# The first batch of an attention and feed-forward kernel rebuilt: weight conversion, softmax division and the second batch's scores

## The chip, the cores and the metric

The kernel runs on one core of one Trainium2 chip. The metric is the device time of one execution in microseconds (us), the median of several runs. The engines are TensorE (PE, matrix products; PEld is its weight load), VectorE (DVE), ScalarE (ACT), GpSimd (POOL) and SyncE (SP, which here only issues transfers). Each runs its own instructions in order and waits for the others by semaphores.

## What is computed

Eight batches of causal windowed attention with eight heads (576 positions, 64 columns a head, a window of 128, a slope of position for each head), then a bilinear feed-forward layer without a nonlinearity. Cut to what matters:

```python
scores = scale * np.matmul(q, k.transpose(0, 1, 3, 2))
scores = np.where(mask, scores + bias[None], -1000000000.0)
scores = scores - np.max(scores, axis=-1, keepdims=True)
attn = np.exp(scores)
attn = attn / (np.sum(attn, axis=-1, keepdims=True) + 1e-09)
attn_out = np.matmul(attn, v)
x = np.ascontiguousarray(attn_out.transpose(0, 2, 1, 3)).reshape(B * S, H * D)   # 4608 x 512
a, b = x @ w_a, x @ w_b                                                          # 512 x 1536 each
out = (a * b) @ w_out                                                            # 1536 x 512
```

The weights arrive as 64-bit floats, and the kernel turns them into 32-bit floats itself. Most products are made of pairs of 16-bit numbers (a high and a low half, three products for one), which needs a power of two as a scale for every operand.

## The kernel before, in words

Heads go in pairs, four pairs to a batch. The scores of a pair are nine tiles of 64 queries by at most 192 keys, laid into four PSUM banks (`BANKS`). The feed-forward layer of a batch is `up` (12 blocks f, each with 48 matmuls of 288 columns in the plain form) and `down` (288 matmuls).

**Batch 0** has its own attention, `first_attention`, in float32. For each bank `first_scores` makes the scores (line 438), subtracts them from the row minimum on DVE (442), takes the exponential with its row sum on ACT (443), adds 1e-9 to the sums (444), takes their reciprocal (445), multiplies the probabilities by it (449 on ACT, 451 on DVE) and transposes them on PE (454). `first_pv` multiplies by v (400), and `keep_x` copies the result out of PSUM (322).

**Weights.** `as_float32` loads one block (512 columns of 128 partitions) and puts together each float from its two words: the low word by ACT (124) or, in every second call, by POOL (126), the high word by DVE (127, 128), the sum by POOL (129). `up_weights` then squares the block (139), sums over the partitions on PE (141), takes a scale (145 and `power_scale`, lines 107 to 110) and splits the block into two halves (152 on ACT, 153 on DVE). `down_weights` does the same for the output weights, with one scale for all (164 to 176). Four of the twelve steps of `up_weights` are woven into the first attention, the rest and `down_weights` into batch 0's `up`.

**Batches 1 to 7.** `attention` is a generator of sevenths of a pair. For each pair it squares q and k for a scale (`qk_squares`, 245 to 248, with a small sum on PE, 256), splits them (`split_qk`, 260 to 263), lays the halves out by four transfers (266 to 269), makes the scores from 16-bit halves (290), normalises the probabilities into two halves, `phl` (307, 308), transposes them by a transfer into `pT` (313), and multiplies by v (400). `v_squares` (211) and `v_scale` (the sum `vtot` on PE, 218) give v's scale once a batch. `Pace.along` spreads these steps along the matmuls of the batch before: while batch b runs `up`, the attention goes to place 4b + 4, while it runs `down`, to 4b + 6.

**What sets the order.** A scheduler orders the instructions of each engine. From batch 1 on, PE's instructions stand in the order in which the code is written; in batch 0 no engine's do.

Of the kernel before, what the change touches and what calls it, by code (L numbers as in the profile page):

```python
# [46 lines left out]
def attention_then_bilinear_ffn(ctx: ExitStack, tc: tile.TileContext, qT, kT, vP, w_a, w_b, w_out, rel, slopes2, outT):  # L47
# [38 lines left out]
    raws = [wdn[:, 2 * n:2 * n + 2, :, :].rearrange("p a c f -> p (a c f)").bitcast(I64) for n in range(6)]  # L86
    forms = [wup[:, n, 4:6, :, :, :].rearrange("p a c k f -> p (a c k f)").bitcast(F32) for n in range(NF)]
# [24 lines left out]
    turn, tt, tt0 = count(), count(), count()  # L112

    def as_float32(x, src):

        k = next(turn)
        raw = raws[k % 6]
        act.dma_start(raw, src)
        words = raw.bitcast(I32).rearrange("p (n two) -> p n two", two=2)
        low, high = words[:, :, 0], words[:, :, 1]  # L120
        t = x.bitcast(I32)

        if k % 2 == 0:
            act.activation(low, low.bitcast(U32), AF.Copy, scale=float(2.0**-29))
        else:
            pool.tensor_scalar(out=low, in0=low.bitcast(U32), scalar1=float(2.0**-29), scalar2=None, op0=ALU.mult)
        vec.tensor_scalar(out=t, in0=high, scalar1=3, scalar2=0x3FFFFFF8, op0=ALU.logical_shift_left, op1=ALU.bitwise_and)
        vec.scalar_tensor_tensor(out=t, in0=high, scalar=-0x40000000, in1=t, op0=ALU.bitwise_and, op1=ALU.bitwise_or)  # L128
        pool.tensor_tensor(out=t, in0=t, in1=low, op=ALU.add)  # L129
        return raw.bitcast(BF16)[:, 0:512]  # L130

    def up_weights(f):

        ps = ps_at.tile([P, 512], F32, tag="at", name="wn_ps")
        fs = []
        for m, w in ((0, w_a), (1, w_b)):
            x = forms[(2 * f + m) % NF]
            sq = as_float32(x, w[f])
            act.activation(sq, x, AF.Square)
            for c in range(NKC):  # L140
                pe.matmul(ps[:, m * P:(m + 1) * P], ones16, sq[:, c * P:(c + 1) * P], start=(c == 0), stop=(c == NKC - 1))
            fs.append(x.rearrange("p (a k f) -> p a k f", a=2, k=2))
            yield
        top = small.tile([P, 2], F32, tag="wtop", name="wtop")
        vec.tensor_reduce(out=top, in_=ps[:, 0:2 * P].rearrange("p (m f) -> p m f", f=P), op=ALU.max, axis=AX)

        power_scale(sup[:, f, :], top, 1.01, 14)
        for m in range(2):
            s = sup[:, f, m:m + 1]

            hi, lo = ((wup[:, f, 0:2, n, :, :] if m == 0 else wup[:, f, 3:1:-1, n, :, :]) for n in range(2))
            act.activation(hi, fs[m], AF.Copy, scale=s)
            vec.scalar_tensor_tensor(out=lo, in0=fs[m], scalar=s, in1=hi, op0=ALU.mult, op1=ALU.subtract)  # L153
        yield

    def down_weights():

        sums = small.tile([P, NF], F32, tag="wos", name="wos", bufs=1)
        for f in range(NF):
            sq = as_float32(forms[f], w_out[f])  # L160
            act.activation(sq, forms[f], AF.Square, accum_out=sums[:, f:f + 1])
            yield
# [9 lines left out]
        vec.tensor_scalar(out=ratio, in0=sab, scalar1=smin, scalar2=so, op0=ALU.mult, op1=ALU.mult)  # L172
        for f in range(NF):
            s = ratio[:, f:f + 1]
            act.activation(wdn[:, f, 0, :], forms[f], AF.Copy, scale=s)
            vec.scalar_tensor_tensor(out=wdn[:, f, 1, :], in0=forms[f], scalar=s, in1=wdn[:, f, 0, :], op0=ALU.mult, op1=ALU.subtract)
            if f % 2:
                yield
# [52 lines left out]

    def load_qk(b, p):
# [19 lines left out]
    def split_qk(o):  # L252
# [10 lines left out]
        vec.scalar_tensor_tensor(out=lo.rearrange("p h s -> p (h s)"), in0=qk.rearrange("p h s -> p (h s)"), scalar=own, in1=hi.rearrange("p h s -> p (h s)"), op0=ALU.mult, op1=ALU.subtract)  # L263

        o.qs = work.tile([P, 2, S], F16, tag="qst", name="qst", bufs=1)
# [8 lines left out]
        vec.reciprocal(o.neg, t)  # L274
        o.bias = work.tile([P, WIN], F32, tag="bias", name="bias")
        eng = vec if b == 1 else pool
        eng.tensor_scalar(out=o.bias, in0=rel_sb, scalar1=t, scalar2=sl2_sb[:, p:p + 1], op0=ALU.mult, op1=ALU.mult)
# [3 lines left out]
    def scores(o, bi):  # L281
# [3 lines left out]
        for i, c in BANKS[bi]:  # L285
            w = TILES[i][1]
            qq, kk = slice(64 * i, 64 * i + 64), slice(64 * i + 64 - w, 64 * i + 64)
            for ks, last in ((o.kh, False), (o.kl, True)):
                for e in range(2):
                    pe.matmul(ps[64 * e:64 * e + 64, c:c + w], o.qs[:, e, qq], ks[:, e, kk], start=not last, stop=last)  # L290
# [452 lines left out]
    for _ in range(10):  # L743
        next(att)
# [75 lines left out]
```

## Time and profile before

| What | us |
|---|---|
| Three runs: median, lowest, highest | 1092.01, 1091.65, 1095.06 |
| The profiled execution: its own time, its span | 1091.0, 1089.2 |
| First `up` matmul of batch 0 | 58.0 |
| First `down` matmul of batch 0 | 216.2 |
| First `up` matmul of batch 1 | 259.6 |
| First `down` matmul of batch 1 | 345.6 |
| Last `down` matmul of batch 1 | 398.7 |

The profile is one execution. Times in it count from the start of its span. The granted clock is the share of its full clock that PE was given. A view by stretches gives the busy time of each engine; a view by groups gives, for a line of the code, the operation, how often it ran, its busy time, the mean duration in ns, and the idle time of the engine ahead of it with what ended it. In names such as `wup<-wdn`, the tile written stands left and the tile read right.

### The profile page before, as it was taken

Reading aid. Unit: us, or ns where it says so; the run is one execution under the profiler, and the core shown is the slowest. Engines: PE = TensorE matmul, PEld = TensorE weight load, DVE = VectorE, ACT = ScalarE, POOL = GpSimd, SP = SyncE. Lnnn points to the kernel's source line nnn. Section 1 sums busy time; section 2 is a strip of 40 time slices with the busy share of each in tenths; the row PEclk is TensorE's granted clock in tenths of the full one; section 3 lists DMA queues with packets and bytes.
Section 4 is the critical chain, followed back from the end, with each engine's and each line's share of the span. In section 5 each row is a group of like instructions: output and inputs, shape, how many; then the busy total and the mean of one; then the engine's idle time right before and its main releaser. Section 6 shows DMA issues by size and latency. Waiting matters only on the chain.

```text
span 1089.2 us, 23914 instructions
## 1 busy us (share of the span) xinstructions
PE 986.8 (91%) x9231; PEld 755.8 (69%) x9231; DVE 725.9 (67%) x2028; ACT 661.6 (61%) x1730; POOL 327.0 (30%) x345
## 2 busy tenths in 40 slices
PE   6776867498999979989799999999999999999998
PEld 5454645376777757767577777777777777777776
DVE  6849998974658845798477758675777666632530
ACT  6957775867546665566656676566756675522321
POOL 6316536500136801496021301122112202220110
PEclk7987988698999989999899999999999999999999
DMA  7236665556323641235431463246334643200000
GB/s 277 78 101 190 200 122 160 130 134 130 66 55 71 145 107 34 51 84 147 110 83 45 100 164 79 61 89 172 81 62 89 154 100 62 40 28 17 2 12 33
DMA packets 149714, 105.19 MB, mean 97 GB/s; under 512 B 120288, under 2 KB 128608, under 8 KB 148576
## 3 DMA queue, kind: packets, MB, share of 16 engines
q1 hardware_dynamic: 134912, 75.25, 31.0%
q10 hardware_dynamic: 14688, 28.42, 8.0%
q8 instruction: 72, 1.18, 0.4%
q14 instruction: 42, 0.34, 0.1%
HBM read 48.33 MB, written 9.44 MB: 53 GB/s over the span
## 4 chain that ended last, share of the span: by engine, by line
PE 43%; DMA 5%; ACT 4%; DVE 2%; issue 1%; ACTq 0%; SPq 0%; DVEq 0%
PE ch L596 15%; PE dn_ps L691 13%; PE p L596 11%; DMA pT<-phl 2%; PE x_ps L400 2%; ACT phl L307 2%; PE sc_ps L290 2%; DMA qk<-in_kT 1%; DMA v<-in_vP 1%; ACT t L295 1%; DVE phl L308 1%; ACT vsq L211 0%; DVE qkl L263 0%; ACT rc L638 0%; DVE rin L303 0%
## 5 line engine op out<-in xcount | busy, mean ns | idle before, releaser
L596 PEld LDWEIGHTS <-wup 128*128 128x128 f16 x4212 | 409.4, 99 | 147.2 <-issue 24.3
L691 PE MATMUL dn_ps<-h,wdn 128*128 128x288 f16 x2304 | 301.3, 290 | 0.0
L691 PEld LDWEIGHTS <-wdn 128*128 128x128 f16 x2304 | 222.6, 99 | 64.7 <-issue 0.5
L596 PE MATMUL ch<-xs,wup 128*128 128x288 f16 x1584 | 229.0, 286 | 5.7 <-DVE rc L655 2.9
L596 PE MATMUL up_ps<-xs,wup 128*128 128x288 f16 x1440 | 193.9, 295 | 18.4 <-DVE wup L153 8.5
L596 PE MATMUL p<-xs,wup 128*128 128x288 f16 x1188 | 178.1, 286 | 5.4 <-ACT rc L638 5.4
L295 ACT ACTIVATE t<-t,mn 128x192 f32<-128x192 f32 (+2 forms) x252 | 107.4, 427 | 63.5 <-DVE mn L294 63.3
L650 POOL TENSOR_TENSOR rc<-rc,row 128x288 f32<-128x288 f32 x66 | 57.2, 866 | 268.2 <-DVE row L648 203.2
L308 DVE SCALAR_TENSOR_TENSOR phl<-t,rin,phl 128x192 f16<-128x192 f32 (+2 forms) x252 | 104.0, 447 | 17.1 <-ACT phl L307 17.0
L307 ACT ACTIVATE phl<-t,rin 128x192 f16<-128x192 f32 (+2 forms) x252 | 88.7, 424 | 23.5 <-DVE rin L304 12.3
L294 DVE CUSTOM_DVE_ANT_0 t<-sc_ps,bias,neg 128x192 f32<-128x192 f32 (+2 forms) x252 | 87.4, 388 | 22.1 <-PE sc_ps L290 21.9
L589 ACT CAST h<-rc 128x576 f16<-128x576 f32 x96 | 64.0, 666 | 57.3 <-DVE rc L655 24.9
L590 DVE TENSOR_TENSOR h<-rc,h 128x576 f16<-128x576 f32 x90 | 74.2, 824 | 23.5 <-ACT h L589 22.6
L329 POOL TENSOR_TENSOR xq<-xq,sq 128x576 bf16<-128x576 bf16 x24 | 34.0, 1417 | 164.8 <-ACT sq L328 164.7
L335 DVE TENSOR_TENSOR xs<-v,xs 128x576 f16<-128x576 f32 x51 | 52.9, 1050 | 27.1 <-ACT xs L334 26.8
L400 PE MATMUL x_ps<-pT,vhl 128*64 128x128 f16 (+3 forms) x1176 | 50.3, 238 | 18.7 <-DMA pT<-phl 17.3
L695 ACT ACTIVATE row<-dn_ps,oi 128x288 f32<-128x288 f32 x64 | 31.5, 492 | 56.1 <-PE dn_ps L691 55.4
L627 DVE TENSOR_TENSOR rc<-p,rc 128x288 f32<-128x288 f32 x66 | 29.9, 454 | 53.1 <-PE p L596 47.9
L400 PEld LDWEIGHTS <-vhl 128*64 128x64 f16 (+1 forms) x1176 | 46.3, 115 | 22.8 <-DMA pT<-phl 17.9
L290 PEld LDWEIGHTS <-qst 128*64 128x64 f16 x1008 | 36.9, 112 | 36.0 <-issue 30.4
L290 PE MATMUL sc_ps<-qkh,qst 128*64 128x192 f16 (+2 forms) x504 | 52.1, 253 | 9.0 <-DMA qkh<-qkh 8.9
L129 POOL TENSOR_TENSOR wup<-wup,wdn 128x512 int32<-128x512 int32 x36 | 50.8, 1416 | 29.7 <-DVE wup L128 10.8
(132 smaller groups left out, 1284.7 us busy)
## 6 DMA issues: line engine op xcount, KB each, us to landing
v<-in_vP SPq DMA_DIRECT2D x8, 1280.0 KB, 6.2
qk<-in_qT SPq DMA_DIRECT2D x32, 288.0 KB, 4.0
qk<-in_kT SPq DMA_DIRECT2D x32, 288.0 KB, 4.4
out<-row ACTq DMA_DIRECT2D x64, 144.0 KB, 1.8
wdn<-in_w_a ACTq DMA_DIRECT2D x12, 512.0 KB, 3.8
wdn<-in_w_b ACTq DMA_DIRECT2D x12, 512.0 KB, 5.2
wdn<-in_w_out ACTq DMA_DIRECT2D x12, 512.0 KB, 5.2
qst<-qkh SPq DMA_DIRECT2D x28, 144.0 KB, 2.8
```

Of the source, the lines that this page charges most:

```text
L290: pe.matmul(ps[64 * e:64 * e + 64, c:c + w], o.qs[:, e, qq], ks[:, e, kk], start=not last, stop=last)
L294: vec.tensor_tensor_reduce(out=t[:, c:c + w], in0=ps[:, c:c + w], in1=o.bias[:, WIN - w:WIN], scale=o.neg, scalar=3.0e38, op0=ALU.add, op1 ...
L295: act.activation(t[:, c:c + w], t[:, c:c + w], AF.Exp, bias=o.mn[:, n:n + 1], scale=-1.0, accum_out=o.sm[:, n:n + 1])
L307: act.activation(phl[:, 0, pc:pc + w], e, AF.Copy, scale=s)
L308: vec.scalar_tensor_tensor(out=phl[:, 1, pc:pc + w], in0=e, scalar=s, in1=phl[:, 0, pc:pc + w], op0=ALU.mult, op1=ALU.subtract)
L335: vec.tensor_tensor(out=xs[:, n, 1, :, :], in0=src, in1=xs[:, n, 0, :, :], op=ALU.subtract)
L400: pe.matmul(xp[oc // 512][64 * h:64 * h + 64, o0:o0 + w], vt[0:rows, c:c + 64], probs(pt, rows, blocks, h), start=(n == 0 and first), stop ...
L589: act.copy(h[:, f, :, 0, :], hid)
L590: eng.tensor_tensor(out=h[:, f, :, 1, :], in0=hid, in1=h[:, f, :, 0, :], op=ALU.subtract)
L596: pe.matmul(ps[:, 0:HT], wup[:, a[0], a[1], wi, k, :], xs[:, b, xi, k, :], start=(first and n == 0), stop=(last and n == len(ks) - 1), ski ...
L650: pool.tensor_tensor(out=x0, in0=x0, in1=mid, op=ALU.mult)
L691: pe.matmul(ps[:, 0:HT], wdn[:, f, wi, e * P:(e + 1) * P], h[:, f, t, hi, :], start=(m == 0 and n == 0), stop=(m == NF - 1 and n == 2))
```

## The change

It rewrites batch 0 and shifts steps of the attention of all others:

- **Weights.** `convert` works on two blocks in one call (128 x 2 x 512), with the low words always on ACT. The steps of a block are spread over four turns, so that one block is converted while the one before is summed and scaled and the one before that is split. Three loads go through SP. In the first attention 2.2 turns are taken for each bank, so that most of the blocks are done there.
- **First attention.** The probabilities stay undivided. A matmul with ones (`ones32`) gives the sums in the layout of x, ACT copies them out, DVE takes a reciprocal of 128 x 576 for each pair, and x is multiplied by it when it is read from PSUM. The scores of a bank are made ahead of the transposes of the bank before.
- **Batch 1's scores** come from float32 q and k, loaded as they are: no squares, no scale, no split, no layout transfers. The bias tile goes from DVE to POOL.
- **Pace.** Batch 0's `up` takes the attention to place 3.5 and its `down` to 4.9 (before: 4 and 6). `first_up` keeps two results waiting before they are read, and `first_down` goes over f outside and the four output blocks inside. In batch 0 SP's transfers stand in written order.
- **All batches.** The third pair (p == 2) of a batch has its products with v and its normalisation later; `v_squares` and `v_scale` come one seventh later; the layout transfers follow the last bank of scores.

```diff
-    def as_float32(x, src):
...
+    def convert(n):
+        low, high, t = words(n)
+        act.activation(low, low.bitcast(U32), AF.Copy, scale=float(2.0**-29))
+        vec.tensor_scalar(out=t, in0=high, scalar1=3, scalar2=0x3FFFFFF8, op0=ALU.logical_shift_left, op1=ALU.bitwise_and)
+        yield
+        vec.scalar_tensor_tensor(out=t, in0=high, scalar=-0x40000000, in1=t, op0=ALU.bitwise_and, op1=ALU.bitwise_or)
+        for m in range(2):
+            pool.tensor_tensor(out=t[:, m, :], in0=t[:, m, :], in1=low[:, m, :], op=ALU.add)
+        yield
...
+        def pv(p, pt):
+            sums = [ps_ch.tile([P, 512], F32, tag="ch", name="sum_ps") for _ in range(2)]
+            each_pv(sums, (ones32,), (pt,))
+            yield
+            r = first.tile([P, S], F32, tag="rin0", name="rin0", bufs=1)
+            x = st.v[:, p, 0:S]
+            for n, (c, w) in enumerate(halves_of_x):
+                act.activation(r[:, c:c + w], sums[n][:, 0:w], AF.Copy, bias=1e-9)
+            xp = [ps_ch.tile([P, 512], F32, tag="ch", name="x_ps") for _ in range(2)]
+            each_pv(xp, (st.v[:, p, :],), (pt,))
+            vec.reciprocal(r, r)
+            yield
+            for n, (c, w) in enumerate(halves_of_x):
+                vec.scalar_tensor_tensor(out=x[:, c:c + w], in0=xp[n][:, 0:w], scalar=st.sv, in1=r[:, c:c + w], op0=ALU.mult, op1=ALU.mult)
...
+            if o.b == 1:
+                for e in range(2):
+                    r = slice(64 * e, 64 * e + 64)
+                    pe.matmul(ps[r, c:c + w], o.q[r, qq], o.k[r, kk], start=True, stop=True)
+                continue
...
+            elif prev and p != 1:
                 prev.vhl = split_v(st, prev.p)
...
-            if o:
+            if o and p != 2:
                 normalize(o)
...
+        weave(att.along(first_up(st, h), 49, 3.5), (weights, 0, 48, 50))
+        weave(att.along(first_down(0, out_scale(st), h), 24, 4.9), (weights, 0, 12, 12))
```

How the instructions stand now, on the two engines that the waits lead to. First DVE in the first attention, around the last bank of a pair. `t` holds a bank's scores, `sm` its row sums, `mn` the row minima, `sup` the scale of a weight block, and `rin` the reciprocals of the sums in the layout of x. Before:

```order
L445 RECIPROCAL sm_285<-sm_285 128x3
L451 TENSOR_SCALAR t_149<-t_149,sm_285 128x64
L451 TENSOR_SCALAR t_149<-t_149,sm_285 128x192
L444 TENSOR_SCALAR sm_312<-sm_312 128x2
L442 ISA t,mn_334<-sc_ps,bias_282 128x192
L442 ISA mn_334 128x1
```

With the change:

```order
L127 TENSOR_SCALAR wup<-wdn 128x2x512
L157 TENSOR_REDUCE wtop<-wn_ps 128x2
L110 TENSOR_SCALAR sup<-r 128x2
L580 RECIPROCAL rin_548<-rin_548 128x576
L550 ISA t,mn_600<-sc_ps,bias_378 128x192
L550 ISA mn_600 128x1
```

The small sums, reciprocals and products between the minima are gone; in their place stand weight instructions of double width, and once a pair a reciprocal of 576 columns.

Second ACT near the end of a `down` (that of batch 1), where v of the next batch is squared. `vsq` is the square of v, `qkl` that of the next pair's q and k, `row` an output block. Before:

```order
L211 ACTIVATE vsq,vs<-v 128x640
L245 ACTIVATE qkl,qs<-qk 128x1152
L295 ACTIVATE t,sm<-t,mn 128x192 x2
L211 ACTIVATE vsq,vs<-v 128x640
L695 ACTIVATE row<-dn_ps,oi 128x288
```

With the change:

```order
L260 ACTIVATE vsq,vs<-v 128x640
L365 ACTIVATE t,sm<-t,mn 128x192
L869 DMA out<-row 128x288
L365 ACTIVATE t,sm<-t,mn 128x192
L260 ACTIVATE vsq,vs<-v 128x640
L365 ACTIVATE t,sm<-t,mn 128x192
L303 ACTIVATE qkl,qs<-qk 128x1152
```

The last square of v now stands ahead of the squares of q and k, and no longer behind them. On PE the sum `vtot` that needs it stands 18 `down` matmuls ahead of the next `up`, where it stood 36 ahead.

More of the change, by code (lines that the diff above doesn't have):

```diff
@@ L1 @@
 from contextlib import ExitStack
-from itertools import chain, count, cycle
+from itertools import chain, cycle
 import numpy as np
@@ L110, in power_scale, with load_weights @@
         vec.tensor_scalar(out=dst.bitcast(I32), in0=r, scalar1=float(-(2**23)), scalar2=float((189 + top) * 2**23), op0=ALU.mult, op1=ALU.add)
-    turn, tt, tt0 = count(), count(), count()
-    def as_float32(x, src):
[L116 to L126, printed above, removed]
+    def load_weights(n, srcs, queue=act):
+        for m, src in enumerate(srcs):
+            queue.dma_start(raws[n % 3][:, m, :], src)
@@ new lines, in first_attention @@
+        bias(0)
+        n = 4 * NPAIR
+        t = exponentials(0, 0, products(0, 0))
+        beside = iter(())
+        for k in range(n):
+            p, bi = k // 4, k % 4
+            ps = products((k + 1) // 4, (k + 1) % 4) if k + 1 < n else None
+            other(0.5)
+            if bi == 1 and p + 1 < NPAIR:
+                bias(p + 1)
+            tp = transposed(t)
+            if ps:
+                t = exponentials((k + 1) // 4, (k + 1) % 4, ps)
+            next(beside, None)
+            keep(bi, tp, pts[p % 2])
+            if p == 0 and bi < 2:
+                v_squares(st, (2 * bi, 2 * bi + 1))
+            if p == 0 and bi == 2:
+                v_scale(st)
+            if bi == 3:
+                beside = pv(p, pts[p % 2])
+            other(0.5)
@@ L502, in first_attention @@
+        for _ in beside:
+            other(0.5)
         states[0] = st
-        yield
     def attention():
@@ L527, in attention @@
                 scores(o, 0)
+            nxt = squares(i + 1)
+            if p == 1 and b > 1:
+                st = load_v(b)
+            if p == 2:
+                late.vhl = split_v(st, late.p)
+            yield i + 1 / 7
+            if o:
+                scores(o, 1)
             if p == 2:
@@ L610, in up_plain @@
                 yield
[L611 removed]
+        halve(hid, f, h, vec)
     def up_fast(st, f, h):
```

355 lines of the change are left out of this document (222 added, 133 removed).

## The prediction

> **What bounds the kernel now.** I read the busy time by stretches first, cut at the stages of the table above.
>
> ```profile
> core 0: us, PE busy (x) PEld busy (x) DVE busy (x) ACT busy (x) POOL busy (x), PEclk, DMA share, GB/s
> 0.00:58.00 58.00, 41.01 (x345) 28.68 (x346) 44.90 (x162) 46.48 (x141) 28.66 (x43) 0.81 0.47 167
> 58.00:200.00 142.00, 104.75 (x922) 75.79 (x920) 121.81 (x304) 95.94 (x237) 68.58 (x44) 0.87 0.57 155
> 200.00:259.60 59.60, 47.65 (x461) 36.15 (x462) 43.40 (x148) 44.15 (x120) 10.84 (x9) 0.83 0.62 136
> 259.60:345.60 86.00, 82.70 (x778) 64.53 (x777) 51.95 (x128) 47.64 (x120) 25.92 (x35) 0.96 0.37 77
> 640.00:755.00 115.00, 112.08 (x1109) 86.74 (x1106) 80.31 (x244) 76.44 (x206) 23.62 (x23) 1.00 0.44 101
> ```
>
> The last row is one batch of the steady part: PE is busy 112 of 115 us, so little is left there. The first three rows are batch 0. It takes 259.6 us where a steady batch takes 115; its most loaded engine is DVE (44.90 + 121.81 + 43.40 = 210 us), with ACT at 187, PE at 193 and a lower clock. From 58 to 200 DVE is busy 122 of 142 us. So batch 0 is set by DVE, with holes, and everything later by PE. Next, what PE waited for, first in batch 0, then after it.
>
> ```profile
> PE x_ps L400 <- DMA pT<-phl: 17.3, 2, 9.2
> PE tr_ps L454 <- ACT t L449: 9.3, 5, 3.6
> PE up_ps L596 <- DVE wup L153: 8.5, 4, 4.0
> PE sc_ps L290 <- DMA qkh<-qkh: 7.0, 2, 4.5
> ...
> PE vtot L218 <- DVE vc L215: 15.9, 5, 6.6
> PE p L596 <- ACT rc L638: 5.4, 10, 1.7
> ```
>
> In batch 0 four different releasers follow each other: the transfer of the probabilities, the division on ACT, the weight split on DVE, the layout transfer. The change touches three of the four. After batch 0 the largest wait is the sum of v's squares, 15.9 us in five pieces.
>
> **Batch 0, what DVE loses.** Busy times are of the first 260 us.
>
> ```profile
> L451 DVE TENSOR_SCALAR t<-t,sm 128x192 f32<-128x192 f32 (+2 forms) x18 | 8.4, 474 | 0.4
> L444 DVE TENSOR_SCALAR sm<-sm 128x2 f32<-128x2 f32 (+1 forms) x16 | 3.8, 240 | 3.5 <-ACT t L443 3.4
> L445 DVE RECIPROCAL sm<-sm 128x2 f32<-128x2 f32 (+1 forms) x16 | 2.6, 161 | 0.2
> L263 DVE SCALAR_TENSOR_TENSOR qkl<-qk,own,qkh 128x1152 f16<-128x1152 f32 x7 | 10.9, 1559 | 2.0 <-ACT qkh L262 1.9
> L277 DVE TENSOR_SCALAR bias<-rel_sb,ninv,sl_sb 128x192 f32<-128x192 f32 x4 | 1.8, 447 | 0.0
> L272 DVE SCALAR_TENSOR_TENSOR ninv<-sc 128x1 f32<-128x1 f32 x7 | 1.1, 150 | 0.0
> ```
>
> - The division of the probabilities (451, 444, 445) goes: 8.4 + 3.8 + 2.6 = **14.8 us**.
> - Batch 1's preparation of q and k goes for four of the seven pairs prepared by then: 4/7 of 10.9 + 1.1 is 6.9, the bias adds 1.8; with seven other instructions a pair of at least the 0.15 us of line 272, 4.2, it is **12.9 us**.
> - Lines 127 and 128 run 18 times in place of 36, at twice the width. The fixed part of an instruction is about that of one element, 0.15 us (line 272): 36 x 0.15 = **5.4 us**.
> - POOL no longer converts low words, and DVE is held up by them:
>
> ```profile
> 16.46 0.69 DVE L128 SCALAR_TENSOR_TENSOR wup<-wdn,wup 128x512 int32<-128x512 int32 x1
> 17.06 0.42 DVE L127 TENSOR_SCALAR wup<-wdn 128x512 int32<-128x512 int32 x1
> 19.09 0.87 DVE L127 TENSOR_SCALAR wup<-wdn 128x512 int32<-128x512 int32 x1
> 18.71 1.88 POOL L126 TENSOR_SCALAR wdn<-wdn 128x512 int32<-128x512 uint32 x1
> L126 POOL TENSOR_SCALAR wdn<-wdn 128x512 int32<-128x512 uint32 x18 | 32.8, 1823 | 49.8 <-DVE wup L127 17.8 <-DVE wup L153 10.5 <-DMA wdn<-in_w_out 8.9
> L127 DVE TENSOR_SCALAR wup<-wdn 128x512 int32<-128x512 int32 x36 | 19.0, 527 | 6.8 <-DMA wdn<-in_w_out 4.7 <-DMA wdn<-in_w_a 2.0
> ```
>
> The same line takes 0.42 us alone and 0.87 beside line 126, 0.53 in the mean, so its 36 runs lose 36 x 0.11 = 4 us. POOL is busy 108 us in batch 0, 33 of them with line 126. Line 127 is a tenth of DVE's time: if only it were held up, 33/108 of 4 is 1 us; if all of DVE were held up alike (210 x 0.11/0.53 = 44 us), 13. I take **6**.
>
> **What DVE gains.** A reciprocal of 576 columns is in no row; the widest is of 12.
>
> ```profile
> L445 DVE RECIPROCAL sm<-sm 128x2 f32<-128x2 f32 x12 | 1.9, 159 | 0.2
> L445 DVE RECIPROCAL sm<-sm 128x3 f32<-128x3 f32 x4 | 0.7, 170 | 0.0
> L166 DVE RECIPROCAL sab<-sab 128x12 f32<-128x12 f32 x1 | 0.2, 215 | 0.0
> L459 DVE COPY pT<-tr_ps 128x512 f32<-128x512 f32 x2 | 1.4, 683 | 0.0
> ```
>
> From 2 to 12 columns it grows by 56 ns, 5.6 a column, against 1.3 a column in all for the copy of 512. Over 576 columns that is 3.4 us. The ends are a copy's price, 0.77, and the steepest pair of rows (2 to 3 columns, 11 ns), 6.5. I take 3.4, the longest step: 4 x 3.4 = **13.6 us** (3 to 26). The product that writes x from PSUM, 512 and 64 columns, is at most 0.9 us by the copy: 4 x 0.9 = **3.6**.
>
> The Trainium skill, "VectorE: DVE Perf Modes", section "First, the fixed hardware budget", speaks against this edit: reciprocal is an iterative divide with a repeat count of 8. At that page's 0.96 GHz an estimate is 576 x 8 / 0.96 = 4.8 us, and the sum would come out 5.6 us higher; the slope over narrow rows agrees with it in kind, not in size.
>
> Sum for DVE: -14.8 - 12.9 - 5.4 - 6 + 13.6 + 3.6 = -21.9. In the timeline above the 128 of 16.46 lasts until 17.15 and runs into the 127 of 17.06: neighbours overlap by about a tenth, so **-20 us**.
>
> **What moves.** By place 4.9 instead of 6, five pairs of scores stand ahead of batch 1 instead of six. A pair costs DVE
>
> ```profile
> L294 DVE CUSTOM_DVE_ANT_0 t<-sc_ps,bias,neg 128x192 f32<-128x192 f32 (+2 forms) x54 | 18.6, 385 | 4.0 <-PE sc_ps L290 4.0
> L308 DVE SCALAR_TENSOR_TENSOR phl<-t,rin,phl 128x192 f16<-128x192 f32 (+2 forms) x54 | 23.8, 484 | 2.1 <-ACT phl L307 2.1
> ```
>
> (18.6 + 23.8) / 6 + 1.6 for its split = 8.7 us: **-9** in batch 0. In batch 1 PE pays for it, and batch 0 pays for the float32 scores:
>
> ```profile
> 31.00:36.00 5.00, 3.36 (x36) 2.39 (x36) 1.00 0.19 40
> 346.40:360.00 13.60, 2.09 (x36) 1.23 (x36) 1.00 0.11 32
> 346.40:360.00 13.60, 1.63 (x42) 1.55 (x42) 1.00 0.11 32
> DVE xs L335 <- ACT xs L334: 8.3, 1, 8.3
> ```
>
> The first row is a pair's scores in float32, the second one in halves, the third a product with v, all at full clock. The moved pair puts 2.1 + 1.6 = **+4 us** on PE in batch 1, where DVE has room (52 of 86 us). Float32 adds 4 x 1.3 = 5 us to PE in batch 0, and the sums by ones about as much again as float32 products with v. PE is busy 193 of 259.6 us there, so most lies beside DVE; for the part in `down`, where PE leads, and for `first_down` reading four banks in a row at its turn, I charge **+3**. If DVE no longer leads, up to 10 are paid.
>
> The fourth row is DVE's longest wait in batch 0, at the seam between first attention and `up`. With most weight blocks now beside the attention and the sums behind, there is other work for DVE in that hole: **-6** (0 to -8). The edits on ACT are costed at nothing: it loses its share of the divisions, the row sums' reads and the squares of q and k, gains the low words of 18 blocks, and stays under DVE (187 against 210); without that cover they cost the difference, a few us. The three loads that go through SP stand ahead of v there; v is first used after the first bank, and a late v costs only that bank's cover.
>
> Batch 0: -20 - 9 - 6 + 3 = **-32 us**; batch 1: +4.
>
> **Batches 1 to 7.** `vtot` stands 18 `down` matmuls later on PE, and 18 of them take 2.3 us:
>
> ```profile
> 616.13 2.31 PE dn_ps L691 x18
> 643.66 0.24 PE L218 MATMUL vtot<-vc,ones 128*128 128x1 bf16 x4 [1.57 <-DVE vc L215]
> 391.27 0.25 PE L218 MATMUL vtot<-vc,ones 128*128 128x1 bf16 x4 [6.59 <-DVE vc L215]
> ```
>
> Three of the five waits are like the 1.57 and vanish, 4 us; the two long ones lose 2.3 each. The 6.59 loses more, because the last square of v stood on ACT behind the squares of q and k and now stands ahead. I take -9 of 15.9. The waits for ACT's copies (5.4 us) come where ACT stands at `phl` and waits for the transfer that still reads it:
>
> ```profile
> 534.72 8.30 DMA pT<-phl
> 543.11 1.50 ACT phl L307 x5
> 545.12 0.90 PE p L596 x6
> ```
>
> The third pair's normalisation now comes two sevenths later: -3. Together **-12** (0 to -20; what is behind PE there is all the rest of its queue).
>
> **Sum**, against the profiled execution's own 1091.0 (1 us under the median): 1091 - 32 + 4 - 12 = **1051 us**.
>
> **The rivals.**
> - *Dearer reciprocals.* Iteration makes one column cost near the upper rows, 8 ns, 4.8 us a pair: 4 x 1.4 more, **1057**. For it the slope; against it the row of 12. The rule of the Trainium skill above is this one.
> - *The waits only change names after batch 0.* PE takes everything in written order there, and a later step can hold what stands behind it: no gain and 4 us lost with the moved pair, 1091 - 32 + 4 + 2 = **1065**. For it: steady batches have 3 us of idle PE, so nothing much can be won.
> - *DVE isn't the bound, the chain is.* Four releasers alternate in batch 0; with each shorter, the next takes over, and half of 32 is won: 1091 - 16 + 4 - 2 = **1077**.
> - *Slower.* DVE's order puts each reciprocal ahead of the next pair's minima; it waits for transposes, sums and the copy. If DVE stands still for that chain, about 8 us a pair (3.4 for the next scores by the row above, as much again for transposes and sums, 1 for copies), that is 32 us, and 12 more if the reciprocals take 6.5: 1091 - 32 + 32 + 12 + 4 - 12 = **1095**. It decides from about 40 us of added DVE time or idle before the first `up`; DVE idles 58.0 - 44.9 = 13 us there now. Against it: the sums are asked for a bank ahead, and weight instructions stand between.
>
> **How the numbers follow.** My forecast 1051 (its own range 1038 to 1062) 0.40; dearer reciprocals 0.12; names only 0.17; chain 0.15, of which 0.02 reaches no change; slower 0.10; no change from a mixture of these 0.03; better than 1035, if the holes of batch 0 close altogether, 0.03. Faster by over 0.3% (about what a measurement of this kernel can tell from no change): 0.40 + 0.12 + 0.17 + 0.13 + 0.03 = 0.85; within it 0.05; slower 0.10. Leaving out the slower case, no change and the very good one (0.16) gives a range of 1035 to 1086.
>
> **What would show it.** Right: `down` of batch 0 starts near 185 instead of 216 and `up` of batch 1 near 228; DVE's busy time to there is near 182; the reciprocal's row shows 3 to 5 us; batch 1 takes some 140 us again; `vtot` waits under 8 us in all. Wrong: an idle DVE in the first 60 us, a first `up` later than 100, reciprocals over 6 us, or a new long wait of PE in the steady batches, above all at the third pair's products with v.

## The result and the profile after

The changed kernel takes 1066.76 us (median of four runs, 1064.65 to 1067.54) where the kernel before takes 1092.22: the ratio, taken of the means, is 0.9759, with a 95% interval of 0.9737 to 0.9781. The forecast was 1051. The profiled execution took 1064.65 us, its span is 1062.9. One execution of the experiment `halves_b1` (1127.68 us) and one of `late_v3_copies` (1997.99) lie far above the others of their kernels and are left out of the ratios below.

The first view is the busy time by stretches, cut at the first matmuls of `up` and `down`. The first cut is at 90.6, where `up` of batch 0 starts in earnest; 18 matmuls of it stand alone, 12 at 67.2 and 6 at 73.9.

```profile
core 0: us, PE busy (x) PEld busy (x) DVE busy (x) ACT busy (x) POOL busy (x), PEclk, DMA share, GB/s
0.00:90.60 90.60, 62.34 (x528) 41.94 (x528) 79.55 (x167) 57.52 (x107) 41.17 (x51) 0.84 0.51 188
90.60:190.60 100.00, 92.28 (x798) 68.00 (x798) 86.23 (x217) 78.09 (x193) 35.15 (x26) 0.93 0.44 127
190.60:234.40 43.80, 42.15 (x422) 32.71 (x421) 19.41 (x69) 23.87 (x66) 5.47 (x5) 1.00 0.49 118
234.40:320.00 85.60, 82.48 (x820) 63.81 (x819) 58.26 (x175) 56.40 (x153) 25.02 (x34) 1.00 0.46 95
320.00:367.80 47.80, 43.46 (x411) 32.35 (x410) 38.56 (x104) 33.61 (x91) 33.53 (x39) 0.96 0.55 135
615.40:731.60 116.20, 113.23 (x1117) 87.55 (x1114) 80.12 (x244) 77.02 (x207) 24.40 (x23) 1.00 0.45 100
```

Batch 0 takes 234.4 us, batch 1 133.4. DVE, with 185.2 us in batch 0, still fills the first attention; behind it PE is busy for 92 and 96% of the time. The steady batch in the last row takes 116.2.

What PE waits for, in batch 0 and then in all that follows, and DVE's new instructions in batch 0 (groups by line and shape):

```profile
PE up_ps L769 <- DVE wup L129: 6.1, 1, 6.1
PE up_ps L769 <- DVE v L583: 5.6, 1, 5.6
PE vtot L267 <- DVE vc L264: 4.3, 1, 4.3
PE up_ps L769 <- DVE pT L565: 4.0, 1, 4.0
...
PE x_ps L474 <- DMA pT<-phl: 1.5, 1, 1.5
```

```profile
PE ch L769 <- ACT rc L794: 6.6, 5, 1.9
PE vtot L267 <- DVE vc L264: 4.4, 2, 2.4
PE ch L769 <- ACT row L805: 3.5, 5, 0.8
PE sc_ps L360 <- DMA qkl<-qkl: 3.1, 6, 1.0
```

```profile
L580 DVE RECIPROCAL rin<-rin 128x576 f32<-128x576 f32 x4 | 15.0, 3741 | 0.0
L583 DVE SCALAR_TENSOR_TENSOR v<-x_ps,sv,rin 128x512 f32<-128x512 f32 x4 | 3.0, 738 | 0.0
```

The wait for the transposed probabilities went from 17.3 to 1.5 us. After batch 0 the sum of v's squares (`vtot`) is waited for 4.4 us where it was 15.9; the 4.3 in batch 0 is its first one, at 21 us. Other waits grow beside these: at `ch` and `p` copies on ACT are waited for 11.3 us (5.8 before), and the layout transfers 4.5 (2.4 before).

Stage by stage (a batch from its first `up` matmul to the next one's; batch 0 from the start), with two of the experiments below between the two kernels, so that each column adds one piece of the change. All are lengths in one profiled execution each.

| Stage | Before | + float32 scores | + all the rest but the pace | Changed |
|---|---|---|---|---|
| Batch 0 | 259.6 | 242.0 | 241.9 | 234.4 |
| Batch 1 | 139.1 | 132.9 | 128.2 | 133.4 |
| Batch 2 | 133.2 | 131.9 | 130.3 | 130.3 |
| Batches 3 to 6 | 456.7 | 456.4 | 466.0 | 464.2 |
| Batch 7 | 100.6 | 100.6 | 100.6 | 100.6 |
| Span | 1089.2 | 1063.8 | 1067.0 | 1062.9 |

The change wins 25.2 us in batch 0, 5.7 in batch 1, 2.9 in batch 2, and loses 7.5 in batches 3 to 6. The same code doesn't give the same lengths twice: four experiments that leave the code from batch 1 on as in the changed kernel (`divide_p`, `recip_twice`, `pool_low`, `rate15`) show 134.5 to 136.7 us for batch 1, 129.8 to 132.0 for batch 2 and 461.8 to 466.5 for batches 3 to 6. So 2 or 3 us in one cell aren't told from nothing.

### The profile page after: what moved, and what is told of

It reads as the page before. It is cut to its first block, busy times and chain, and to the rows that moved or that the text cites. A ratio compares the mean times of both kernels' runs of the same rounds, so it can differ in the third digit from the quotient of the medians.

```text
span 1062.9 us, 23801 instructions
## 1 busy us (share of the span) xinstructions
PE 989.0 (93%) x9291; PEld 756.1 (71%) x9291; DVE 711.3 (67%) x1918; ACT 645.7 (61%) x1636; POOL 305.5 (29%) x332
## 4 chain that ended last, share of the span: by engine, by line
PE 42%; DVE 5%; ACT 4%; DMA 4%; issue 1%; ACTq 0%; SPq 0%; DVEq 0%
PE ch L769 14%; PE dn_ps L864 14%; PE p L769 11%; PE x_ps L474 2%; PE sc_ps L360 2%; ACT phl L377 2%; DMA qk<-in_kT 2%; DMA v<-in_vP 1%; DVE phl L378 1%; DVE qkl L321 1%; DMA pT<-phl 1%; ACT qkh L320 1%; DVE t L364 0%; DVE r L109 0%; ACT vhl L277 0%
## 5 line engine op out<-in xcount | busy, mean ns | idle before, releaser
L864 PE MATMUL dn_ps<-h,wdn 128*128 128x288 f16 x2016 | 258.9, 287 | 2.3 <-DVE h L763 2.0
L864 PEld LDWEIGHTS <-wdn 128*128 128x128 f16 x2016 | 192.9, 98 | 56.3 <-issue 2.6
L769 PE MATMUL up_ps<-xs,wup 128*128 128x288 f16 x1440 | 187.9, 291 | 18.4 <-DVE wup L129 6.1
L378 DVE SCALAR_TENSOR_TENSOR phl<-t,rin,phl 128x192 f16<-128x192 f32 (+2 forms) x252 | 110.4, 477 | 17.1 <-ACT phl L377 16.4
L364 DVE CUSTOM_DVE_ANT_0 t<-sc_ps,bias,neg 128x192 f32<-128x192 f32 (+2 forms) x216 | 75.4, 390 | 13.5 <-PE sc_ps L360 13.3
L408 DVE TENSOR_TENSOR xs<-v,xs 128x576 f16<-128x576 f32 x51 | 52.5, 1039 | 22.5 <-ACT xs L407 22.3
L868 ACT ACTIVATE row<-dn_ps,oi 128x288 f32<-128x288 f32 x56 | 27.5, 491 | 51.2 <-PE dn_ps L864 50.4
L805 ACT ACTIVATE row<-ch,g 128x288 f32<-128x288 f32 x66 | 32.6, 494 | 41.5 <-PE ch L769 41.0
L828 DVE SCALAR_TENSOR_TENSOR rc<-rc,g,ch 128x288 f32<-128x288 f32 x66 | 33.6, 509 | 34.7 <-PE ch L769 34.5
L234 POOL TENSOR_TENSOR wa<-wup 128x512 f32<-128x512 f16 x24 | 33.1, 1380 | 66.8 <-DVE phl L378 61.0
L360 PEld LDWEIGHTS <-qst 128*64 128x64 f16 x864 | 30.4, 109 | 29.8 <-issue 28.1
```

Source lines behind the costliest of these rows:

```text
L364: vec.tensor_tensor_reduce(out=t[:, c:c + w], in0=ps[:, c:c + w], in1=o.bias[:, WIN - w:WIN], scale=-0.125 if o.b == 1 else o.neg, scalar= ...
L378: vec.scalar_tensor_tensor(out=phl[:, 1, pc:pc + w], in0=e, scalar=s, in1=phl[:, 0, pc:pc + w], op0=ALU.mult, op1=ALU.subtract)
L408: vec.tensor_tensor(out=xs[:, n, 1, :, :], in0=src, in1=xs[:, n, 0, :, :], op=ALU.subtract)
L769: pe.matmul(ps[:, 0:HT], wup[:, a[0], a[1], wi, k, :], xs[:, b, xi, k, :], start=(first and n == 0), stop=(last and n == len(ks) - 1), ski ...
L864: pe.matmul(ps[:, 0:HT], wdn[:, f, wi, e * P:(e + 1) * P], h[:, f, t, hi, :], start=(m == 0 and n == 0), stop=(m == NF - 1 and n == 2))
```

## The experiments

Ratios are against the kernel before; the changed kernel's is 0.9759 (0.9737 to 0.9781), so 0.001 is 1.1 us.

**The float32 scores alone, in the kernel before** (`before_f32`).

```diff
-                qks[i] = load_qk(1 + i // NPAIR, i % NPAIR)
+                qks[i] = (load_plain_qk if i < NPAIR else load_qk)(1 + i // NPAIR, i % NPAIR)
...
+            if o.b == 1:
+                for e in range(2):
+                    r = slice(64 * e, 64 * e + 64)
+                    pe.matmul(ps[r, c:c + w], o.q[r, qq], o.k[r, kk], start=True, stop=True)
+                continue
```

> The kernel before, with only batch 1's scores made from float32 q and k (loaded as they are; bias on POOL). Theory A (this part carries most of the gain by itself): 12 to 23 us faster than before, all of it ahead of batch 1's up; undoing the same part in the changed kernel took 21 to 23. Rival B (it is worth what was forecast for it, 12.9 us of DVE less some 5 of PE): 5 to 10 us faster. Rival C (it pays only where the first attention is short, because before, the transfers and divisions of the first attention are waited for anyway): under 4 us.

1066.94 us, ratio 0.9762 (0.9739 to 0.9786): Theory A, but with 6.2 of its 25.4 us of span in batch 1, not all ahead of it. This one part gives what the whole change gives. Batch 0 by stretches, before and with the part, and what PE then waits for:

```profile
0.00:259.60 259.60, 193.41 (x1726) 140.62 (x1727) 210.11 (x613) 186.56 (x495) 108.09 (x96) 0.85 0.56 154
```

```profile
0.00:242.00 242.00, 194.82 (x1722) 142.28 (x1723) 194.40 (x574) 177.35 (x483) 113.67 (x100) 0.89 0.55 157
```

```profile
PE tr_ps L473 <- ACT t L468: 10.0, 7, 3.1
PE qtot L268 <- DVE both L257: 8.6, 2, 6.2
PE x_ps L419 <- DMA pT<-phl: 4.8, 2, 2.5
```

DVE is busy 15.7 us less (third busy column), and the batch is 17.6 shorter. PE's busy time hardly moves. The wait for the transposed probabilities falls from 17.3 to 4.8 us and that for `qkh`, 7.0, is gone; a part comes back as a wait for the squares of batch 2's q and k (`both`, from 3.3 to 8.6). No run separates the transfers from DVE's work; both go with this part.

**The same part undone in the changed kernel** (`halves_b1`): the same edit the other way round.

> The changed kernel, with batch 1's scores made from 16-bit halves again (squares, scale, split and layout transfers of four pairs come back). Theory A (DVE's and ACT's time sets batch 0): 10 to 15 us slower, since 12.9 us of DVE work come back, and layout transfers are waited for again. Rival B (PE has become the bound from the first up on): 0 to 5 us faster, since float32 scores cost PE 1.3 us a pair more. Between them, near 0, if PE's gain and DVE's loss cancel.

Ratio 0.9956 (0.9935 to 0.9977), 21.5 us slower, beyond Theory A's range; batch 0 takes 257.3 us, 22.9 more, and DVE's busy time there is 197.1, only 11.9 more. The rest is waiting:

```profile
PE sc_ps L355 <- DMA qkh<-qkh: 9.6, 1, 9.6
PE up_ps L765 <- DVE v L578: 8.2, 1, 8.2
PE x_ps L469 <- ACT rin L572: 7.1, 3, 3.3
```

The layout transfer is waited for again. The other two stand in the first attention, whose work is the same; no engine but SP has a written order there, so the scheduler placed it differently. How much of the 22.9 is that stays open.

**The old pace in batch 0** (`pace46`).

```diff
-        weave(att.along(first_up(st, h), 49, 3.5), (weights, 0, 48, 50))
-        weave(att.along(first_down(0, out_scale(st), h), 24, 4.9), (weights, 0, 12, 12))
+        weave(att.along(first_up(st, h), 49, 4), (weights, 0, 48, 50))
+        weave(att.along(first_down(0, out_scale(st), h), 24, 6), (weights, 0, 12, 12))
```

> The changed kernel, with the old places of the attention in batch 0: to 4 beside up and to 6 beside down, so six pairs of scores stand ahead of batch 1 and not five. Theory A (the forecast: the pair moved off batch 0 saves 9 us of DVE there and costs PE 4 in batch 1): 3 to 7 us slower. Rival B (DVE is busy for only 19 of the 44 us of batch 0's down, so the pair costs PE alone, wherever it stands): the down of batch 0 4 to 8 us longer, the down of batch 1 as much shorter or more, within 2 us in all.

Ratio 0.9778 (0.9757 to 0.9799), 2 us slower, which the intervals don't part. By stages batch 0 is 7.5 us longer and batch 1 5.2 shorter. Batch 0's `down`, with the part above in the kernel before and here, and what PE waits for in the second:

```profile
199.40:242.00 42.60, 42.60 (x383) 32.27 (x382) 28.77 (x97) 33.06 (x92) 2.63 (x3) 0.94 0.68 153
```

```profile
190.80:241.90 51.10, 45.58 (x413) 33.22 (x412) 26.30 (x102) 30.22 (x88) 5.04 (x6) 0.93 0.56 128
```

```profile
PE dn_ps L751 <- ACT rc L722: 2.7, 1, 2.7
PE dn_ps L751 <- ACT row L755: 2.4, 1, 2.4
```

`up` ends where it does in the changed kernel (190.8 and 190.6); the whole difference is in this `down`, 51.1 us against 43.8, as Rival B says; batch 1 gets it back mostly in its `up` (81.8 against 85.6), not in its `down`. DVE is busy for only 26.3 of the 51.1: what the new pace saves is 3.4 us of PE's work and these waits for ACT's copies, which the changed kernel doesn't have. The row for all of batch 0 shows what the rest of the change does there:

```profile
0.00:241.90 241.90, 197.77 (x1787) 142.20 (x1788) 197.43 (x504) 169.98 (x398) 82.29 (x83) 0.92 0.52 156
```

Beside the row of the float32 scores alone, the rebuilt first attention, the weight chain, POOL's lost work, the new order of steps and `first_up`/`first_down` together leave batch 0 at 241.9 instead of 242.0, with DVE 3.0 us *busier*. By the two rows of `down` the first `down` matmul comes 8.6 us earlier, and `down` is 8.5 longer. The new order of steps has a share in the second: alone in the kernel before it makes that `down` 5.2 longer (48.6 against 43.4).

**Probabilities divided again in the changed kernel** (`divide_p`).

```diff
-                act.activation(e, e, AF.Exp, bias=mn[:, n:n + 1], scale=-1.0)
+                act.activation(e, e, AF.Exp, bias=mn[:, n:n + 1], scale=-1.0, accum_out=sm[:, n:n + 1])
+            vec.tensor_scalar(out=sm[:, 0:m], in0=sm[:, 0:m], scalar1=1e-9, scalar2=None, op0=ALU.add)
+            vec.reciprocal(sm[:, 0:m], sm[:, 0:m])
...
-            vec.reciprocal(r, r)
```

> The changed kernel, with the probabilities of the first batch divided before they are transposed, as before (row sums on ACT, 16 small sums and reciprocals and half the divisions on DVE, the other half on ACT; no matmuls with ones, no reciprocals of 576 columns, x copied out by ACT). DVE loses 4 x (3.74 + 1.01) = 19.0 us and gets 14.8 back. Theory A (DVE's time sets the first attention): 2 to 6 us faster, so this part of the change costs time. Rival B (the division stands in the chain between exponential and transpose, where PE waited 9.3 us before): 4 to 10 us slower. Rival C (no difference): the scores made a bank ahead hide the division, and DVE's 4 us are hidden too.

Ratio 0.9782 (0.9765 to 0.9799), not parted from the changed kernel's; batch 0 takes 237.3 us, 2.9 more, though DVE is busy 6.7 us less (178.5). So Theory A falls; the 2.9 lie between B and C. The chain shows in PE's waits:

```profile
PE tr_ps L567 <- DVE t L561: 20.8, 9, 4.8
```

**A second reciprocal** (`recip_twice`).

```diff
             vec.reciprocal(r, r)
+            vec.reciprocal(r, r)
```

> The changed kernel, with each reciprocal of 128 x 576 run a second time in place, so that x is multiplied by the sums and not divided by them. It adds 4 x 3.74 = 15.0 us of DVE time, all of it ahead of the first up in earnest. Theory A (DVE sets the first attention: it is busy 79.6 of the first 90.6 us): 12 to 15 us slower, the first up later by as much. Rival B (the chain of transposes, sums and copies sets it, DVE has room): under 5 us slower. Rival C (a late first up is made good later, since weights are further on by then): the first up later by 12 to 15, but the end by half of it.

Batch 0, changed and with the second reciprocal:

```profile
0.00:234.40 234.40, 196.77 (x1746) 142.65 (x1747) 185.20 (x452) 159.47 (x365) 81.78 (x82) 0.91 0.48 149
```

```profile
0.00:250.80 250.80, 199.93 (x1746) 145.07 (x1747) 191.38 (x456) 159.29 (x365) 80.67 (x82) 0.86 0.45 139
```

Ratio 0.9889 (0.9859 to 0.9918), 14.2 us slower, and batch 0 is 16.4 longer for 15.0 us of added reciprocals. That is Theory A in size, though `up` starts in earnest 21.0 us later (111.6), beyond its range. But DVE's busy time grows by only 6.2 us: the 24 splits of weights and the `phl` products of 128x192, the same instructions in both, take 10.0 us less here (why is shown at the end). And a reciprocal is also a link from the sums to x, which `up` waits for, so the run doesn't tell DVE's load from the chain's length.

**Low words on POOL again** (`pool_low`).

```diff
-        act.activation(low, low.bitcast(U32), AF.Copy, scale=float(2.0**-29))
+        if n % 2 == 0:
+            act.activation(low, low.bitcast(U32), AF.Copy, scale=float(2.0**-29))
+        else:
+            for m in range(2):
+                pool.tensor_scalar(out=low[:, m, :], in0=low[:, m, :].bitcast(U32), scalar1=float(2.0**-29), scalar2=None, op0=ALU.mult)
```

> The changed kernel, with every second call's low words on POOL again (18 instructions of 1.8 us, 33 us of POOL time, 10 us taken off ACT). In the trace, DVE instructions that run into one of POOL's last 1.1 us longer, whatever their size. Theory A (POOL holds DVE up, and DVE sets the first attention): DVE's time in batch 0 grows by 6 to 12 us, and the kernel is 6 to 12 slower. Rival B (ACT was as near to the bound as DVE, and is relieved): within 2 us. Rival C (the chain through POOL, low word, sum, square, gets longer by 1.8 - 1.15 us a block and sets the blocks' pace): slower, with DVE's busy time unchanged.

```profile
0.00:235.80 235.80, 196.26 (x1745) 142.67 (x1746) 185.49 (x452) 149.72 (x356) 115.08 (x100) 0.90 0.48 148
```

Ratio 0.9782 (0.9766 to 0.9798). POOL is busy 33 us more in batch 0, DVE 0.3, and the batch takes 1.4 longer: Theory A falls. Rivals B and C aren't told apart.

**A slower weight chain** (`rate15`).

```diff
-        first_attention(weights, 2.2)
+        first_attention(weights, 1.5)
```

> The changed kernel, with 1.5 turns of the weights for each bank of the first attention in place of 2.2, so about a third of the weight work moves from beside the first attention to beside up. Theory A (DVE's total sets batch 0, wherever the work stands): the first up in earnest 8 to 15 us earlier, the start of batch 1 within 3 us of 234. Rival B (up then waits for its weights, f by f): the start of batch 1 later by 4 to 10. Rival C (the work fills DVE's idle time in up and down): earlier by 4 to 8.

Ratio 0.9774 (0.9747 to 0.9801). `up` starts in earnest at 85.8 instead of 90.6, and batch 1 at 235.6 instead of 234.4: where the weights stand hardly matters, as Theory A says, though `up` came less early than it says.

**The old order of steps in the changed kernel, and the new one in the kernel before** (`old_order`, `before_new_order`). The loop of `attention` is exchanged; its core, seen from the changed kernel:

```diff
-            if p == 2:
-                late.vhl = split_v(st, late.p)
...
+            if p == 2:
+                pv(late.p, st, late, late.vhl)
+                transpose_probs(prev)
```

> The changed kernel, with the steps of the attention of batches 1 to 7 in the order of before. Theory A (the new order wins the vtot waits, 9 us, and pays them back in waits for ACT's copies and for the layout transfers): the waits only change names, so the time is 1063 to 1067, 0 to 4 us under the changed kernel; batches 2 to 6 take what they took before, 116 us, and the last up 72 instead of 77. Rival B (the order wins what was forecast): 1075 to 1080, 8 to 14 us slower. Rival C (the loss in the late batches comes from the attention being further behind after a place of 4.9 in batch 0, and not from the order): the same time within 2 us, and the last up stays at 77.

> The kernel before, with only the new order of steps in the attention of batches 1 to 7. Theory A (waits change names after batch 0, but in batch 1 the wait of 6.6 us for v's squares and the slow clock behind it, 3 us, go): 1083 to 1090, 2 to 9 us faster, nearly all of it in batch 1 and the start of batch 2. Rival B (the forecast): 12 us faster or more, spread over batches 1 to 7. Rival C (the order costs in every steady batch): 1 to 6 us slower.

Old order: ratio 0.9787 (0.9765 to 0.9810), not parted from the changed kernel by its time. By stages the new order is worth 8.9 us in batch 1 (142.3 against 133.4) and 2.8 in batch 2, and costs 1.6 in batch 0 (232.8 against 234.4) and 5.2 in batches 3 to 6 (459.0 against 464.2); the last long `up` is back at 72.9 (77.1), as Theory A says. No theory had both signs. New order alone: 0.9968 (0.9946 to 0.9991), 3.5 us faster: Theory A in size, but not in its places. Batch 1 takes 125.8 instead of 139.1 and batch 2 is 3.0 shorter, while batch 0 is 6.0 longer (265.6) and batches 3 to 6 together 6.3 (463.0). A part of the gain in batch 1 is thus paid in batch 0, and the cost in the late batches shows in both kernels.

**Only v's squares and scale early again** (`v_early`).

```diff
+            if p == 1:
+                v_squares(st, (0, 1))
             yield i + 4 / 7
...
             if p == 1:
-                v_squares(st, (0, 1))
+                v_squares(st, (2, 3))
...
             if p == 1:
-                v_squares(st, (2, 3))
+                v_scale(st)
             yield i + 6 / 7
...
             if p == 1:
-                v_scale(st)
                 late = prev
```

> The changed kernel, with only the squares and the scale of v a seventh earlier again; the third pair's later products and normalisation stay. Theory A (the late scale of v is what puts two splits of v on ACT ahead of the first copy of an up): the late ups fall back to 72 or 73 us from 75, and the downs grow by the vtot waits, 1.5 us each and 4 to 9 in batches 1 and 2: 3 to 10 us slower in all. Rival B (the third pair's later normalisation is what makes the ups longer): the ups stay at 74 to 77 and the downs grow all the same, 10 to 16 us slower. Rival C (the long wait in the down of batch 1 goes with the third pair's order): about the same time.

Ratio 0.9747 (0.9724 to 0.9770), the changed kernel's within the intervals. Batch 5's `up` and `down`, changed and with v early:

```profile
731.60:806.30 74.70, 71.48 (x706) 55.77 (x704) 54.62 (x150) 48.70 (x127) 15.15 (x16) 1.00 0.38 81
806.30:847.90 41.60, 41.60 (x412) 31.77 (x410) 25.75 (x94) 27.61 (x78) 9.15 (x7) 1.00 0.50 129
```

```profile
734.90:807.10 72.20, 71.17 (x707) 55.70 (x705) 52.88 (x143) 46.39 (x122) 15.14 (x16) 1.00 0.40 82
807.10:850.60 43.50, 41.70 (x412) 31.73 (x410) 27.10 (x101) 29.60 (x84) 9.14 (x7) 1.00 0.50 129
```

The `up` gets 2.5 us shorter and the `down` 1.9 longer: Theory A's mechanism, but its sum comes out even. ACT at the start of that `up`, changed and with v early, shows how:

```profile
733.38 1.55 ACT L277 ACTIVATE vhl<-v,sv 128x640 f16<-128x640 f32 x2 [0.55 <-DVE sv L110]
734.83 0.48 ACT L868 ACTIVATE row<-dn_ps,oi 128x288 f32<-128x288 f32 x1
735.72 0.40 ACT L794 COPY rc<-ch 128x288 f32<-128x288 f32 x1 [0.41 <-ACT row L868]
```

```profile
734.56 0.82 ACT L277 ACTIVATE vhl<-v,sv 128x640 f16<-128x640 f32 x1
736.17 0.40 ACT L795 COPY rc<-ch 128x288 f32<-128x288 f32 x1 [0.41 <-PE ch L770]
```

With the late scale, two splits of v stand at the start of `up`, and the first `ch` is copied 4.1 us after that start instead of 1.3.

**Two mixtures.** `hybrid4` takes the old loop where `b > 4`. `late_v3_copies` keeps v late only where `b <= 3`, and changes the copies of the transposed probabilities:

```diff
-                (vec.tensor_copy if bi % 2 else act.copy)(pt[:, 4 * bi - 2:4 * bi + 2, :], tp.rearrange("k (b q) -> k b q", q=P))
+                act.copy(pt[:, 4 * bi - 2:4 * bi + 2, :], tp.rearrange("k (b q) -> k b q", q=P))
```

> The changed kernel, with the new order of steps for the attention of batches 1 to 4 and the old one for batches 5 to 7. From the stage lengths of the changed kernel and of the one with the old order: the new order wins 9 us in the down of batch 1 and 4 in that of batch 2, where the sum vtot was waited for longest and the clock fell to a half behind it; after that a down wins 1.4 to 1.7 and the up behind it loses 1.8 to 4.2, through the copies on ACT at its start. Theory A (both hold, place by place): 4 us faster than the changed kernel, 1062 to 1064, the up of batch 6 back at 72 to 73 us. Rival B (the gain in the early batches hangs on the order of the later ones, or the losses are set elsewhere): within 1 us of the changed kernel.

> The changed kernel with two edits at places that the stage lengths keep apart. First, v's squares and scale stand late only for batches 1 to 3, and as before for batches 4 to 7: from the stage lengths measured, the late place wins 3.5 us in the down of batch 1 and 2.6 in that of batch 2, where it costs 3.5 in the up behind, and loses 0.3 to 2.1 a batch after that. Second, all copies of the transposed probabilities of the first attention are on ACT, so DVE loses 8 x 0.68 = 5.4 us ahead of the first up and ACT gains 4.6. Theory A (DVE sets the first attention one for one, as the second reciprocal showed, and the order's gains and losses belong to their places): batch 0 is 4 to 7 us shorter, batches 1 to 6 together 3 to 5 us; 1055 to 1060 in all. Rival B (ACT takes over in the first attention): batch 0 within 2 us of 234 or longer, the rest 3 to 5 us shorter; 1060 to 1065. Rival C (the order's gain is lost again, as in the kernel with the old order from batch 5 on): batches 1 to 6 within 1 us of the changed kernel's.

`hybrid4`: 0.9750 (0.9732 to 0.9768); its last long `up` is 73.2, but the `downs` of its batches 1 and 3 to 5 are 1.6 to 2.8 us longer and a half-clock stretch fell into batch 3: Rival B in sum. `late_v3_copies`: 0.9748 (0.9717 to 0.9780). Batches 1 to 7 are 2.9 us shorter than in the changed kernel, near Theories A and B; batch 0 takes 236.7, 2.3 more, with DVE busy 4.7 us *less* (180.5), which is Rival B. No version is shown to beat the changed kernel.

## Why the prediction was right in direction and too high in gain

- **Preparation of batch 1's q and k, -12.9.** Right in mechanism, too small: DVE -15.7 and batch 0 -17.6, plus 6.2 in batch 1, and alone as much as the whole change. The step that mis-sized it priced only DVE's time, although the rows quoted at its start had the two transfer waits, 17.3 and 7.0, that shrink with it. How much of the gain is the transfers and how much DVE stays open.
- **The rest of batch 0**: division, fewer calls, POOL, reciprocals, product, hole and PE, -14.8 - 5.4 - 6 + 13.6 + 3.6 - 6 + 3 = -12 before overlap. **This is the step that failed.** With the old pace and the new order of steps it gave 0.1 us of batch 0: 8.6 ahead of the first `down`, lost again in that `down`, where PE waits 5.1 us for ACT's copies and where the new order has a share. The sum has no term for either but the +3. By groups of lines in batch 0 (float32 scores alone against the old pace run), the weight lines (127 and 128, now 127 and 129) went from 52.5 to 39.1 us and the division's 14.5 went, as forecast. But 15.0 of reciprocals, 3.7 of products and 2.6 of four more copies of transposed probabilities came, which line 565 now gives to DVE for two banks a pair and the prediction overlooked; and the 54 products of `phl`, unchanged, took 27.4 us instead of 21.8, because more of them were held by POOL (below): of the 42 of 128x192, nine took over 0.55 us, each ending 204 to 220 ns behind the end of a POOL instruction, where only three took that long before, 0.69 to 0.80. POOL's term, -6, is 0.3 of DVE by the run with the low words on POOL. On PE the float32 scores cost 1.4 us and not 5, but the sums by ones take 12.6 in the changed kernel.
- **"Sum for DVE" as the measure of batch 0.** It came near only for the float32 scores alone. With the second reciprocal DVE's time grew by 6.2 us and the batch by 16.4; with the division put back, and with the copies on ACT, DVE's time fell by 6.7 and 4.7 and the batch got 2.9 and 2.3 longer. DVE's busy time also holds time in which POOL kept it waiting, so a row's price isn't fixed. For the rest of the change the rival "the chain sets it" fits better. That what counts is work standing between two waits of PE is the reading that fits; it wasn't isolated.
- **Reciprocals, 3.4.** 3.74 us measured. The dearer price of the Trainium skill, "VectorE: DVE Perf Modes", section "First, the fixed hardware budget", worked out as 4.8, isn't borne out here: 3.74 us for 576 columns is 6.5 ns a column.
- **The moved pair, -9 and +4.** Near in size, -7.5 and +5.2, but by another way, so partly by luck: the -9 is DVE's time, and the 7.5 lies in `down`, where DVE is half idle, as PE's work and PE's waits for ACT.
- **Batches 1 to 7, -12.** -8.9 and -2.8 in batches 1 and 2, then +5.2: the rival "the waits only change names" is right from batch 3 on, where the change even costs. The split was wrong too. Setting the v-early run between the two orders, v's late scale gives -3.0, -2.4 and +5.9 (forecast -9), and the third pair's later steps, forecast at -3, give -5.9, -0.4 and -0.7; the last two are inside the spread named above. All but the long waits of batches 1 and 2 was moved from `down` to the next `up`.
- **What was left out.** A wait of PE was priced at its own length, without the half clock behind it (below).

Of the signs named: `down` of batch 0 started at 190.6 (185 forecast), batch 1 at 234.4 (228), batch 1 takes 133.4 us (some 140), DVE's time to its start is 185.2 (182), and `vtot` waits 4.4 us (under 8), or 8.7 with the one in batch 0, where the kernel before has 16.9. The sign of failure came true as well: new waits in the steady batches, though at the copies of `ch` and not at the third pair's products. That 1066.8 lies beside the 1065 of "names only" is partly chance: batch 0 won 7 us less than that rival has it, and batches 1 and 2 more.

## What to carry to other kernels

Work that disappears with its transfers and its waits is worth more than its busy time; work exchanged for other work on the same engine should be counted line by line, moved copies included, before it is given any gain. An engine's busy time can hold waiting for another engine, so the same instructions can cost 10 us more in one run than in the next. Before moving a step later to spare PE a wait, look at what it sets off on the next engine: here the scale of v spared PE 1.9 us and put two splits ahead of a copy that PE needed. Undo or add each part alone: here one of five edits gave as much as all five.

## What the hardware showed

**A wait costs more than its length.** The stretches around the longest `vtot` wait of the kernel before (PEclk is the third number from the end):

```profile
382.00:384.70 2.70, 2.68 (x22) 2.00 (x21) 2.70 (x10) 2.70 (x8) 0.00 (x0) 1.00 0.16 24
384.70:387.40 2.70, 0.00 (x0) 0.00 (x0) 1.60 (x6) 2.10 (x8) 0.50 (x1) 0.95 0.97 248
387.40:391.30 3.90, 0.03 (x2) 0.03 (x2) 0.75 (x4) 3.14 (x9) 0.00 (x0) 0.50 0.53 150
391.30:397.60 6.30, 6.30 (x32) 4.03 (x32) 3.36 (x9) 2.92 (x7) 0.00 (x0) 0.52 0.10 31
397.60:398.70 1.10, 1.10 (x12) 0.88 (x10) 0.00 (x0) 0.00 (x0) 0.00 (x0) 1.00 0.00 0
```

The wait of 6.59 us is followed by 6.3 us of matmuls at a clock of 0.52, which cost 6.3 x 0.48 = 3.0 us more. The Trainium skill, "TensorE: Matmul & The Clock Gate", section "What's actually happening", has the array fall to half its clock after an idle window of some 3.4 us. The trace agrees on the half; here it set in within 2.7 us of the last matmul, and lasted through 6.3 us of sustained work, where the page gives at least one such window of 3.4.

Summed over stretches of 1 us (busy time by one minus the clock), PE lost 32 us to the clock in the kernel before and 18 in the changed one, of which 23 and 15 in batch 0.

**POOL can hold up a DVE instruction, even a tiny one.** In the changed kernel:

```profile
93.66 3.49 POOL L131 TENSOR_TENSOR wup<-wup,wdn 128x512 int32<-128x512 int32 x2
95.93 1.24 DVE L109 TENSOR_SCALAR r<-cl 128x2 int32<-128x2 int32 x1
97.09 0.75 DVE L408 TENSOR_TENSOR xs<-v,xs 128x576 f16<-128x576 f32 x1
```

Two columns took 1.24 us and ended at 97.17, when POOL's pair ended (93.66 + 3.49 = 97.15). The same line took 0.15 for one column at 733.00, with POOL idle. It is no single case. In batch 0 of the changed kernel seven instructions of lines 109 and 110 took 0.63 to 1.26 us, and each ended 24 to 27 ns behind the end of a POOL instruction; no other took more than 0.21. Of the 35 `phl` products of 128x192, 29 took 0.35 to 0.42 us and ran beside no POOL instruction; six took 1.38 to 1.45 and each ended 215 to 218 ns behind the end of one. So DVE was held until POOL's instruction was over, up to 1.1 us, and this counts as busy time. In the run with the second reciprocal only three of the 35 were held. The Trainium skill, "SBUF — State Buffer", section "Terms", describes such a block: DVE and GpSimd share a pair of ports that is held for a whole instruction. Yet in the run with the low words on POOL, 33 us more of POOL work cost DVE only 0.3 us in sum; no run here isolates which instructions hold each other.
